# Six weight conversions moved among the early products of experts 1 to 3

## Chip, cores and metric

One core of one Trainium2 chip runs the whole kernel. The metric is device time in microseconds (us), as the median of several executions; the less the better. TensorE does matrix products, VectorE, ScalarE and GpSimd work on vectors, and SyncE issues the transfers (DMAs) between memory and the core's SBUF.

## What is computed

The input is q, k and v of 4 batches, 8 heads, 576 positions and 64 channels. Attention keeps the 32 highest scores of every row. Its output, 2304 rows of 512 channels, goes through 8 experts whose mixing weights are balanced by 8 rounds of Sinkhorn scaling:

```python
scores = scale * np.matmul(q, k.transpose(0, 1, 3, 2))
kth = np.partition(scores, -32, axis=-1)[..., -32:-31]
scores = np.where(scores >= kth, scores, -1e9)
attn = softmax(scores) @ v                       # -> x: (2304, 512)
P = np.exp(x @ w_gate - max)
for _ in range(8):
    P /= P.sum(1, keepdims=True) + 1e-09
    P /= P.sum(0, keepdims=True) + 1e-09
    P *= N / E
for e in range(8):
    out += P[:, e:e + 1] * (np.maximum(x @ w1[e], 0.0) @ w2[e])
```

## The kernel before

The rows of x are cut into blocks of 256 rows (two tiles of 128) by batch and phase; one more block gathers the last 64 positions of the batches. Attention makes these blocks stage by stage (`STAGES`), four head pairs to a stage, and each head pair `hp` fills one of the four 128-deep slices of `xts`, so a product that reads slices 0 and 1 needs head pairs 0 and 1 alone. In attention VectorE finds the 32 highest of each row (`topk`, lines 140 and 143), ScalarE copies scores out of PSUM (line 130) and takes exponentials (148, 149), GpSimd normalises (152, 156) and splits keys and queries, and TensorE does scores (121, 122), transposes (241) and the weighted sums (255, 256). Every finished slice of a block that is due is "boarded": split into a high and a low part, `xh` by ScalarE (line 80) and `xl` by VectorE (line 89).

The experts run as 24 visits, `visit(v, on)` with expert `v % 8`. Visits 0 to 3 have block 0 alone, block 1 boards at visit 4, block 2 at visit 8, and so on. While attention still runs, visits give TensorE work between attention's steps. A visit needs the expert's weights converted: `convert` loads a raw tile `wr`, ScalarE makes the high part `wh` (line 80), GpSimd the low part `wl` (line 86). There are three raw buffers, taken in turn by everything that loads weights, and six buffers each of `wh` and `wl`; a raw buffer is free again when the last reader of its tile is done:

```python
WR, WB, XR, NS, RAW, YB = 3, 6, 3, 3, 3, 4
```

Block 0 has an early part, before its four slices are there. `first_quarter` (products on line 490) multiplies slice 0 with raw weights of experts 4 to 7, one tile to an expert. `first_half` (products on line 502) does slices 0 and 1 for experts 0 to 3, two half tiles `half_weights` to an expert (loads on line 473), with 16 matmul instructions to each half. Both copy their results out by ScalarE (line 478) and store them as partial sums `PART` (line 480). Visits 0 to 3 then need `w1`'s other half only: `second_half` loads the partial sum (line 508), does the products on line 454 and adds (line 514); visit outputs are line 563 and their copies line 571.

The early parts are called from the first stage, ahead of head pairs 1 and 2, at a priority below attention's. The order of instructions on each engine is fixed when the kernel is built, by a planner that weighs priorities and its own estimates of durations. Ahead of head pair 2 stands, before `first_half`, the conversion of all six weight tiles of visit 0: two halves of `w1` and four tiles of `w2` (their loads are on line 436).

Of the kernel before, what the change touches and what calls it, by code (L numbers as in the profile page):

```python
# [48 lines left out]
def kernel(  # L49
# [29 lines left out]
    def hi_act(dst, src):  # L79
        nc.scalar.activation(dst, src, AF.Copy)  # L80
# [4 lines left out]
    def lo_pool(dst, src, hi):  # L85
        nc.gpsimd.tensor_tensor(dst, src, hi.bitcast(F32), op=OP.subtract)  # L86
# [240 lines left out]
    def attend_stage(b, phases, mix):  # L327
        xts = {}
        for ph in phases:
            xts[ph] = xp.tile([128, KD, 256], F32, name="xt", bufs=XR)  # L330
            for t in range(2):
                X["t", b, 2 * ph + t] = xts[ph][:, :, t * 128:(t + 1) * 128]
        xm = None
        if mix:
            m = ("m", b // 2 * 2, b // 2 * 2 + 1)
            if m not in X:
                X[m] = xp.tile([128, KD, 128], F32, name="xm", bufs=2)
                mixed[m] = 0
            xm = X[m][:, :, (b % 2) * 64:(b % 2) * 64 + 64]
            mixed[m] += 1  # L340
        for hp in range(HP):
            if (b, phases) == (0, (0,)) and hp in (1, 2):
                with tc.high_priority(offset=-BIG):
                    if hp == 1:
                        first_quarter(xts[0])
                    else:
                        ready[0] = visit_weights(0)
                        first_half(xts[0])
            attend_heads(b, hp, phases, xts, xm)
        for ph in phases:  # L350
            t = tile_id["t", b, 2 * ph]
            if 2 * b + ph == PARKED:
                nc.sync.dma_start(parked, xts[ph])
            gate_logits(xts[ph], [t, t + 1])
        if mix and mixed[m] == 2:
            gate_logits(X[m], [tile_id[m]])
# [10 lines left out]
    def gate_logits(xt, tiles):  # L367
        lp = pst.tile([128, 512], F32, name="pt")
        for i in range(len(tiles)):
            for kk in range(KD):  # L370
                nc.tensor.matmul(lp[:, i * E:(i + 1) * E], xt[:, kk, i * 128:(i + 1) * 128],
                                 wgs[:, kk * E:(kk + 1) * E], start=(kk == 0), stop=(kk == KD - 1))
        m = len(tiles)
        nc.scalar.activation(lg[:, tiles[0]:tiles[0] + m, :].rearrange("p t e -> p (t e)"),
                             lp[:, 0:m * E], AF.Copy)
# [10 lines left out]
    seats = {i: Seat(xh, xl, hh, hl, i * 256) for i in range(2)}  # L386
# [47 lines left out]
    def convert(src, shape):  # L434
        wr = wp.tile(shape, F32, name="wr", bufs=WR)
        nc.sync.dma_start(wr, src)
        return split_weights(wr, shape)

    def split_weights(wr, shape):
        wh = wp.tile(shape, F32R, name="wh", bufs=WB)  # L440
        wl = wp.tile(shape, F32R, name="wl", bufs=WB)
        hi_act(wh, wr)
        lo_pool(wl, wr, wh)
        return wh, wl

    def products(ps, f0, seat, n, wh, wl, k0):
        nk = wh.shape[1]
        cs = slice(seat.c0, seat.c0 + n)
        for fo in range(512 // n):
            fs = slice((f0 + fo) * 128, (f0 + fo + 1) * 128)  # L450
            i = 0
            for kk in range(nk):
                for a, x in ((wh, seat.xh), (wh, seat.xl), (wl, seat.xh)):
                    nc.tensor.matmul(ps[:, fo, :], a[:, kk, fs], x[:, k0 + kk, cs],  # L454
                                     start=(i == 0), stop=(i == 3 * nk - 1))
                    i += 1
# [13 lines left out]
    def half_weights(e, s2, half):  # L470
        wr = wp.tile([128, 2, 2, 256], F32, name="wr", bufs=WR)
        for r in range(2):
            nc.sync.dma_start(wr[:, r], w1[e, 2 * s2 + r, :, 2 * half:2 * half + 2, :])
        return wr

    def part(e, s, ps):
        y = op_.tile([128, 512], F32, name="y", bufs=YB)
        nc.scalar.activation(y, ps.rearrange("p a b -> p (a b)"), AF.Copy)
        PART[e, s] = dram.tile([128, 512], F32, name=f"p{e}_{s}")
        nc.sync.dma_start(PART[e, s], y)  # L480

    def first_quarter(x):
        for e in LATER:
            wr = wp.tile([128, 4, 256], F32, name="wr", bufs=WR)
            for s in range(4):
                nc.sync.dma_start(wr[:, s], w1[e, s, :, 0, :])
            for s in range(4):
                ps = ps1.tile([128, 2, 256], F32, name="p1")
                for fo in range(2):
                    nc.tensor.matmul(ps[:, fo, :], wr[:, s, fo * 128:(fo + 1) * 128], x[:, 0, :],  # L490
                                     start=True, stop=True)
                part(e, s, ps)

    def first_half(x):
        for e in ALONE:
            for s2 in range(2):
                wr = half_weights(e, s2, 0)
                for r in range(2):
                    ps = ps1.tile([128, 2, 256], F32, name="p1")
                    for fo in range(2):  # L500
                        for kk in range(2):
                            nc.tensor.matmul(ps[:, fo, :], wr[:, r, kk, fo * 128:(fo + 1) * 128], x[:, kk, :],  # L502
                                             start=(kk == 0), stop=(kk == 1))
                    part(e, 2 * s2 + r, ps)

    def second_half(e, s, seat, wh, wl, k0):
        y = op_.tile([128, 512], F32, name="y", bufs=YB)
        nc.sync.dma_start(y, PART[e, s])
        y = y.rearrange("p (a b) -> p a b", a=2)
        ps = ps1.tile([128, 2, 256], F32, name="p1")  # L510
        products(ps, 0, seat, 256, wh, wl, k0)
        ft = slice(2 * s, 2 * s + 2)
        with tc.high_priority(offset=2 * BIG):
            nc.vector.tensor_tensor(ps, ps, y, op=OP.add)
            store_hidden(seat, ft, slice(0, 256), ps)
# [5 lines left out]

    ready = {}

    def visit_weights(e):
        w1s = []
        for s2 in range(2):
            wh, wl = split_weights(half_weights(e, s2, 1), [128, 2, 2, 256])
            w1s += [(wh[:, r], wl[:, r]) for r in range(2)]
        return w1s, [convert(w2[e, s], [128, 2, 512]) for s in range(4)]

    def visit(v, on):
        e = v % E
        ids = [SEAT[blk] for blk in on]
        groups = []
        if on[0] == 0:
            on_first, ids = True, ids[1:]
        else:
            on_first = False
        if 0 in ids and 1 in ids:
            groups, ids = [(seats[0], 512)], [i for i in ids if i > 1]  # L540
        groups += [(seats[i], 256) for i in ids]
        if groups:
            for s in range(4):
                wh, wl = convert(w1[e, s], [128, KD, 256])
                if on_first:
                    second_half(e, s, seats[0], wh[:, 1:4], wl[:, 1:4], 1)
                for seat, n in groups:
                    hidden(seat, n, s, wh, wl)
            ws = [convert(w2[e, s], [128, 2, 512]) for s in range(4)]
        else:  # L550
            w1s, ws = ready.pop(v) if v in ready else visit_weights(e)
            for s, (wh, wl) in enumerate(w1s):
                second_half(e, s, seats[0], wh, wl, 2)
        for blk in on:
            seat = seats[SEAT[blk]]
            for ti, piece in enumerate(BLOCKS[blk]):
                ts = slice(seat.c0 + ti * 128, seat.c0 + (ti + 1) * 128)
                ps = ps2.tile([128, 512], F32, name="p2")
                i = 0
                for ft in range(NFT):  # L560
                    wh, wl = ws[ft // 2]
                    for a, m in ((seat.hh, wh), (seat.hh, wl), (seat.hl, wh)):
                        nc.tensor.matmul(ps, a[:, ft, ts], m[:, ft % 2, :],  # L563
                                         start=(i == 0), stop=(i == 3 * NFT - 1))
                        i += 1
                output(v, tile_id[piece], ps)
# [272 lines left out]
```

## Time and profile before

| | |
|---|---|
| median of 3 runs | 1937.91 us (1937.78 to 1939.51) |
| profiled execution, own time | 1935.34 us |
| its span, first to last instruction | 1933.6 us |
| TensorE busy | 1879.3 us |
| VectorE, ScalarE, GpSimd busy | 1320.0, 1110.0, 1015.6 us |
| mean granted TensorE clock | 0.993 |

The profile is one execution. Times in it count from the first instruction. PE is TensorE (PEld its weight loads, which overlap PE), DVE VectorE, ACT ScalarE, POOL GpSimd, SP SyncE. The granted clock is given as a share of full speed, 2.4 GHz; its other level is 1.2 GHz. `L86` is line 86 of the kernel. In a row, what stands in brackets is how long the engine was idle before it and what ended that idle time.

### The profile page before, as it was taken

The numbers are of one execution on the slowest core, as the hardware profiler recorded it, in microseconds if no ns is written. First come the engines' busy times: TensorE is split into PE (matmuls) and PEld (weight loads), VectorE is DVE, ScalarE is ACT, GpSimd is POOL, SyncE is SP. The second block draws the span as 40 slices with busy tenths as digits, with TensorE's granted clock in tenths as the row PEclk, the third lists the DMA queues.
The fourth block names the chain that finished last, engine by engine and source line by source line (L and its number), as shares of the span: only waits on it lengthen the run. The fifth ranks groups of instructions, "written<-read, shape, count | busy, mean of one in ns | idle before, by whom it ended". The sixth has DMA issues, their size and how long they took to land.

```text
span 1933.6 us, 27187 instructions
## 1 busy us (share of the span) xinstructions
PE 1879.3 (97%) x9649; PEld 1578.9 (82%) x9649; DVE 1320.0 (68%) x2645; ACT 1110.0 (57%) x1929; POOL 1015.6 (53%) x778
## 2 busy tenths in 40 slices
PE   5799999999999999999999999999999999999998
PEld 3577788899888888888888888888888888888886
DVE  8979898999898998289999623135555555543333
ACT  5877777777786877578777654443333333333331
POOL 3537766546545535454435488865555445555440
PEclk9899999999999999999999999999999999999999
DMA  4765554434333334343323225633333333211111
GB/s 126 264 222 176 196 160 151 143 108 161 109 124 124 111 101 132 128 138 126 114 93 122 99 78 194 199 120 104 104 109 114 116 103 104 93 60 56 65 33 44
DMA packets 96073, 237.93 MB, mean 123 GB/s; under 512 B 10816, under 2 KB 15040, under 8 KB 95936
## 3 DMA queue, kind: packets, MB, share of 16 engines
q1 hardware_dynamic: 95936, 236.19, 38.0%
q8 instruction: 76, 1.25, 0.3%
q14 instruction: 61, 0.50, 0.1%
HBM read 201.54 MB, written 34.60 MB: 122 GB/s over the span
## 4 chain that ended last, share of the span: by engine, by line
PE 91%; ACT 2%; DMA 2%; POOL 2%; issue 1%; DVE 1%; SPq 0%; ACTq 0%; POOLq 0%
PE p L563 20%; PE p L454 20%; PE p L733 18%; PE p L674 9%; PE pc L674 5%; PE pt L241 3%; PE pb L674 2%; PE sp L121 2%; PE sp L122 2%; PE pt L255 2%; PE pt L279 2%; PE pt L278 2%; PE p L502 2%; DMA wr<-in_w_dram 1%; POOL wl L86 1%
## 5 line engine op out<-in xcount | busy, mean ns | idle before, releaser
L86 POOL TENSOR_TENSOR wl<-wr,wh 128x1024 fp32r<-128x1024 f32 x280 | 674.6, 2421 | 577.2 <-ACT wh L80 524.9
L80 ACT ACTIVATE wh<-wr 128x1024 fp32r<-128x1024 f32 x280 | 295.5, 1061 | 306.4 <-PE p L674 194.0
L140 DVE MAX8 m<-w 128x8 f32<-128x576 f32 x432 | 319.3, 751 | 3.2
L454 PE MATMUL p<-xh,wh 128*128 128x256 f32 (+1 forms) x800 | 271.4, 340 | 0.8 <-DVE hl L519 0.8
L454 PE MATMUL p<-xh,wl 128*128 128x256 f32 (+1 forms) x800 | 271.1, 339 | 0.0
L454 PE MATMUL p<-xl,wh 128*128 128x256 f32 (+1 forms) x800 | 271.1, 339 | 0.0
L563 PE MATMUL p<-wh,hh 128*128 128x512 f32 x640 | 251.4, 396 | 3.5 <-ACT hh L518 3.5
L563 PE MATMUL p<-wl,hh 128*128 128x512 f32 x640 | 250.9, 395 | 0.0
L563 PE MATMUL p<-wh,hl 128*128 128x512 f32 x640 | 244.9, 395 | 0.0
L143 DVE MATCH_REPLACE8 w<-m,w 128x576 f32<-128x576 f32 x288 | 213.5, 742 | 0.1
L580 DVE SCALAR_TENSOR_TENSOR acc<-p,P,acc 128x512 f32<-128x512 f32 x120 | 89.5, 750 | 166.9 <-PE p L733 166.9
L733 PE MATMUL p<-wh,h2h 128*128 128x512 f32 x512 | 199.8, 391 | 1.3 <-ACT h2h L697 0.7
L733 PE MATMUL p<-wl,h2h 128*128 128x512 f32 x512 | 199.9, 391 | 0.0
L733 PE MATMUL p<-wh,h2l 128*128 128x512 f32 x512 | 196.7, 390 | 0.0
L519 DVE SCALAR_TENSOR_TENSOR hl<-p,hh 128x512 fp32r<-128x512 f32 x160 | 109.0, 683 | 97.0 <-ACT hh L518 95.9
L454 PEld LDWEIGHTS p<-xh,wh 128*128 128x128 f32 x800 | 152.5, 191 | 17.1 <-DVE hl L519 1.3
L454 PEld LDWEIGHTS p<-xl,wh 128*128 128x128 f32 x800 | 152.5, 191 | 15.3
L454 PEld LDWEIGHTS p<-xh,wl 128*128 128x128 f32 x800 | 152.4, 191 | 14.2 <-issue 0.4
L563 PEld LDWEIGHTS p<-wh,hh 128*128 128x128 f32 x640 | 120.4, 189 | 26.6 <-ACT hh L518 4.5
L563 PEld LDWEIGHTS p<-wh,hl 128*128 128x128 f32 x640 | 120.3, 188 | 22.4
L563 PEld LDWEIGHTS p<-wl,hh 128*128 128x128 f32 x640 | 120.6, 188 | 22.0
L140 DVE MAX8 m<-s 128x8 f32<-128x576 f32 x144 | 108.2, 751 | 39.8 <-ACT s L130 24.4
(185 smaller groups left out, 3905.9 us busy)
## 6 DMA issues: line engine op xcount, KB each, us to landing
wr<-in_w_dram SPq DMA_DIRECT2D x240, 512.0 KB, 3.5
y<-y SPq DMA_DIRECT2D x160, 256.0 KB, 2.6
raw<-in_k_dram SPq DMA_DIRECT2D x56, 288.0 KB, 3.2
raw<-in_q_dram SPq DMA_DIRECT2D x32, 256.0 KB, 3.3
p<-y SPq DMA_DIRECT2D x32, 256.0 KB, 4.1
wr<-in_w_dram SPq DMA_DIRECT2D x32, 256.0 KB, 3.5
y<-p SPq DMA_DIRECT2D x32, 256.0 KB, 4.7
raw<-in_v_dram SPq DMA_DIRECT2D x20, 288.0 KB, 3.0
```

The source lines that it names most:

```text
L80: nc.scalar.activation(dst, src, AF.Copy)
L86: nc.gpsimd.tensor_tensor(dst, src, hi.bitcast(F32), op=OP.subtract)
L121: nc.tensor.matmul(o, qc, kh[:, cs], start=(i == 0), stop=False)
L140: nc.vector.max(m8[:, u, r, :], ws[u] if r else units[u][0])
L143: nc.vector.match_replace(ws[u], m8[:, u, r, :], ws[u] if r else units[u][0], LOWEST)
L241: nc.tensor.transpose(ps[:, r, :], Ef[:, o:o + 128], idt)
L454: nc.tensor.matmul(ps[:, fo, :], a[:, kk, fs], x[:, k0 + kk, cs], start=(i == 0), stop=(i == 3 * nk - 1))
L519: nc.vector.scalar_tensor_tensor(seat.hl[:, ft, cs], src, 0.0, seat.hh[:, ft, cs].bitcast(F32), op0=OP.max, op1=OP.subtract)
L563: nc.tensor.matmul(ps, a[:, ft, ts], m[:, ft % 2, :], start=(i == 0), stop=(i == 3 * NFT - 1))
L580: return nc.vector.scalar_tensor_tensor(ACC[t], y, g, ACC[t], op0=OP.mult, op1=OP.add)
L674: nc.tensor.matmul(ps, w[:, kk, :], x[:, kk, :], start=(fresh and i == 0), stop=(i == 5), skip_group_check=True)
L733: nc.tensor.matmul(ps, a[:, ft, ts], m[:, ft, :], start=(i == 0), stop=(i == 11))
```

## The change

The six conversions of visit 0 are no longer made ahead of `first_half`. `first_half` makes them itself and returns them: none behind expert 0, and two behind each of experts 1, 2 and 3. The turn in which tiles take the three raw buffers changes from "experts 4 to 7; six conversions; eight halves of experts 0 to 3" to "experts 4 to 7; two halves of expert 0; two of expert 1; two conversions; two of expert 2; two conversions; two of expert 3; two conversions". `visit_weights(e)` becomes `conversion(e, i)`, which makes one of the six; the other visits without a second block call it six times in the same order as before.

```diff
                     if hp == 1:
                         first_quarter(xts[0])
                     else:
-                        ready[0] = visit_weights(0)
-                        first_half(xts[0])
+                        ready[0] = first_half(xts[0])
...
     def first_half(x):
+        got = []
         for e in ALONE:
             for s2 in range(2):
                 wr = half_weights(e, s2, 0)
...
                     part(e, 2 * s2 + r, ps)
+            if e:
+                got += [conversion(0, 2 * e - 2), conversion(0, 2 * e - 1)]
+        return got
...
-    def visit_weights(e):
-        w1s = []
-        for s2 in range(2):
-            wh, wl = split_weights(half_weights(e, s2, 1), [128, 2, 2, 256])
-            w1s += [(wh[:, r], wl[:, r]) for r in range(2)]
-        return w1s, [convert(w2[e, s], [128, 2, 512]) for s in range(4)]
+    def conversion(e, i):
+        if i < 2:
+            return split_weights(half_weights(e, i, 1), [128, 2, 2, 256])
+        return convert(w2[e, i - 2], [128, 2, 512])
...
-            w1s, ws = ready.pop(v) if v in ready else visit_weights(e)
-            for s, (wh, wl) in enumerate(w1s):
-                second_half(e, s, seats[0], wh, wl, 2)
+            got = ready.pop(v) if v in ready else [conversion(e, i) for i in range(6)]
+            for s in range(4):
+                wh, wl = got[s // 2]
+                second_half(e, s, seats[0], wh[:, s % 2], wl[:, s % 2], 2)
+            ws = got[2:]
```

## Rows read from the trace of the kernel before

**Rows 1.** The page: busy us (share of span) and instructions, by engine.
```profile
PE 1879.3 (97%) x9649; PEld 1578.9 (82%) x9649; DVE 1320.0 (68%) x2645; ACT 1110.0 (57%) x1929; POOL 1015.6 (53%) x778
```

**Rows 2.** Stretches: start:end, length, busy us by engine, granted clock, DMA share, GB/s.
```profile
75.25:85.31 10.06, 1.33 (x5) 0.99 (x5) 10.06 (x24) 9.97 (x17) 8.61 (x6) 0.58 0.84 273
85.31:91.20 5.89, 5.89 (x16) 4.80 (x17) 5.89 (x15) 2.27 (x5) 5.81 (x6) 0.56 0.63 202
91.20:135.33 44.13, 44.13 (x232) 34.97 (x231) 37.54 (x83) 29.34 (x60) 13.41 (x18) 1.00 0.68 221
135.33:253.00 117.67, 112.14 (x634) 88.98 (x633) 103.06 (x222) 89.88 (x163) 84.33 (x64) 0.99 0.59 192
253.00:400.00 147.00, 140.00 (x940) 129.16 (x939) 138.17 (x297) 113.02 (x208) 81.54 (x80) 0.98 0.44 143
400.00:1934.00 1534.00, 1526.19 (x7624) 1284.88 (x7622) 958.34 (x1864) 814.75 (x1384) 795.18 (x578) 1.00 0.34 109
```

**Rows 3.** TensorE's timeline, 72 to 136 us: start, duration, instruction.
```profile
72.27 1.03 PE L490 MATMUL p<-xt,wr 128*128 128x256 f32 x4
...
80.36 0.61 PE L121 MATMUL sp<-kh,qs 128*128 128x288 f32 x1 [5.12 <-ACT s L130]
...
85.31 6.25 PE L502 MATMUL p<-xt,wr 128*128 128x256 f32 x16 [3.62 <-DMA wr<-in_w_dram]
...
115.22 0.40 PE L121 MATMUL sp<-kh,qs 128*128 128x288 f32 x1
...
115.85 3.62 PE L502 MATMUL p<-xt,wr 128*128 128x256 f32 x16
...
135.33 0.47 PE L454 MATMUL p<-xh,wh 128*128 128x256 f32 x1
```

**Rows 4.** Lines 80 and 86, 60 to 100 us: ns min/median/max, first and last start.
```profile
L80 ACT ACTIVATE wh<-wr x6: 1039/1091/1098, 63.6 to 82.6; 128x1024 fp32r<-128x1024 f32 x6
...
L86 POOL TENSOR_TENSOR wl<-wr,wh x6: 2356/2364/2381, 64.8 to 86.7; 128x1024 fp32r<-128x1024 f32 x6
```

**Rows 5.** SyncE's timeline, 46 to 112 us: raw weight loads issued.
```profile
57.73 1.26 SPq L473 DMA_DIRECT2D wr<-in_w_dram  x2
...
65.69 0.81 SPq L473 DMA_DIRECT2D wr<-in_w_dram  x2
...
69.98 0.38 SPq L436 DMA_DIRECT2D wr<-in_w_dram  x1
...
82.63 3.53 SPq L473 DMA_DIRECT2D wr<-in_w_dram  x4
```

**Rows 6.** ScalarE's timeline: head pair 1's slice of x written.
```profile
69.57 0.38 ACT L257 ACTIVATE xt<-pt 128x256 f32<-128x256 f32 x1 [1.50 <-PE pt L256]
```

**Rows 7.** Line 473's 24 loads, 50 to 140 us, from issue to landing.
```profile
DMA to landing us min/median/max: 2.5/3.5/5.2
```

**Rows 8.** VectorE's timeline: boarding of slices, and a top-k step.
```profile
72.51 2.40 DVE L89 TENSOR_TENSOR xl<-xt,xh 128x256 fp32r<-128x256 f32 x1 [1.09 <-ACT xh L80]
...
101.41 0.76 DVE L140 MAX8 m<-s 128x8 f32<-128x576 f32 x1 [1.90 <-ACT s L130]
...
107.78 0.43 DVE L89 TENSOR_TENSOR xl<-xt,xh 128x256 fp32r<-128x256 f32 x1 [2.12 <-ACT xh L80]
...
129.33 0.43 DVE L89 TENSOR_TENSOR xl<-xt,xh 128x256 fp32r<-128x256 f32 x1 [1.75 <-ACT xh L80]
...
236.44 0.36 DVE L89 TENSOR_TENSOR xl<-xt,xh 128x256 fp32r<-128x256 f32 x1
```

**Rows 9.** GpSimd's timeline: a conversion at 72 us.
```profile
72.26 2.37 POOL L86 TENSOR_TENSOR wl<-wr,wh 128x1024 fp32r<-128x1024 f32 x1 [2.83 <-ACT wh L80]
```

**Rows 10.** ScalarE's timeline: the last output of visit 3 copied out.
```profile
253.49 0.60 ACT L571 ACTIVATE y<-p 128x512 f32<-128x512 f32 x1
```

**Rows 11.** TensorE's timeline, 315 to 320 us: two waits.
```profile
315.51 0.55 PE L241 MATMUL pt<-idt,Et 128*128 128x128 f32 x3 [1.38 <-DVE atl L89]
318.58 0.55 PE L241 MATMUL pt<-idt,Et 128*128 128x128 f32 x3 [2.52 <-DVE atl L89]
```

## The prediction

> **What bounds the kernel now.** I began with the page's busy times: TensorE is busy for 1879.3 of the 1933.6 us [rows 1], so only some 54 us can be had by filling its gaps, and a change that adds no arithmetic has to be judged by which gaps it fills. Next, the stretches. From 400 us on TensorE is busy 1526.19 of 1534.00 us; from 91.20 to 135.33 it is busy without a break; the gaps that this diff can touch lie between 75.25 and 91.20 [rows 2]. In the first 10.06 us of that it worked 1.33 us, at a granted clock of 0.58, while VectorE and ScalarE were full [rows 2]. TensorE's timeline names the two gaps: 5.12 us until the scores of head pair 2, whose score buffer had to be copied out first, and 3.62 us until the raw weights of `first_half` landed [rows 3]. Then the clock was still at the lower level (0.56, which is mostly 1.2 GHz): the first 16 products of `first_half` took 6.25 us, and the same 16 took 3.62 us at 115.85 [rows 2, 3].
>
> Why the weights landed so late is told by the conversions and SyncE's queue. Six conversions, each 1.09 us on ScalarE and 2.36 us on GpSimd, ran from 63.6 to 89.1 us [rows 4], and all six stand ahead of `first_half` in the three raw buffers. Loads of the first two were issued at 57.73 and 65.69, of the third at 69.98, and the first load of `first_half` only at 82.63 [rows 5]. Yet the rows that these products read, head pairs 0 and 1, were written at 69.57 + 0.38 = 69.95 us [rows 6]. So there was TensorE work whose inputs were ready some 15 us before its weights.
>
> **What the stretch loses.** 10.06 - 1.33 = 8.73 us idle. The four score products cost 1.33 us there and 0.63 us at full clock (from 115.22 to the next row at 115.85), so 0.70 us. The first 16 products: 6.25 - 3.62 = 2.63 us. Together 12.1 us [rows 2, 3]. From 75.25 to 135.33, where visit 0 begins [rows 3], 60.08 us pass with 48.0 us of full-clock work in them.
>
> **The change, part by part.** *Moved loads and products.* In the three raw buffers expert 0's two halves now stand directly behind experts 4 to 7, where two conversions stood. They inherit those issue slots, 57.73 and 65.69, and with the longest landing of such a load, 5.2 us [rows 5, 7], both are there by 71. Expert 1's first half takes the buffer of expert 7, whose last products ended at 72.27 + 1.03 = 73.30 [rows 3]: it lands by 78.5. Each half is 16 products, 3.62 us; expert 1's second half takes the buffer of expert 0's first, free at about 75.25 + 3.62 = 78.9, and lands by 84.1. So four halves, 14.5 us of work, stand in the stretch that held 8.73 us of gaps, each before it is due. I count the 12.1 us as removed in that place, the clock's part with them since no gap is left to lower it.
>
> *Moved conversions.* The same six pairs of instructions and the same loads, two behind each of experts 1, 2 and 3. No instruction is added: 6 x 1.09 = 6.5 us of ScalarE and 6 x 2.36 = 14.2 us of GpSimd go from the front into 91.20 to 135.33, where GpSimd is busy 13.41 of 44.13 us and ScalarE 29.34 [rows 2]. That room hides them: nil. Without it they would be 14.2 us of GpSimd in front of visit 0. Their last need is late: visit 0's first products at 135.33 less the gain, and the four of `w2` later. The weight values, the store order of the partial sums and the later visits (which get the same six conversions in the same order) are unchanged: nil.
>
> *New waits.* Expert 2's first half must now wait for expert 1's second, and its second half for a conversion; expert 3's likewise. With nothing else to do TensorE would wait a load's landing at each, 3.5 us as the median, 5.2 at most [rows 7]: 7.0 to 10.4 us. Behind such a wait stand, in TensorE's queue, the transposes and scores of head pairs 2 and 3; in ScalarE's the score copies and exponentials behind a conversion whose load is late; in GpSimd's the normalising of weights; in SyncE's the next key and query loads. Attention fills part of it: 48.0 - 8 x 3.62 = 19 us of the stretch's work is not `first_half`.
>
> *What is late next.* Filling the gap does not start visit 0 by itself. Visit 0's first products need head pair 3 boarded, which VectorE ended at 129.33 + 0.43 = 129.76 [rows 8]. If attention runs as before, visit 0 starts 135.33 - 129.76 = 5.6 us earlier and the other 6.5 us become idle time ahead of it. That is the lower bound of the gain in this mechanism. Above it stands what attention may gain: boarding head pair 1 took 2.40 us instead of 0.43, beside a conversion on GpSimd that ran from 72.26 for 2.37 us [rows 8, 9], and it now has no conversion beside it: 1.97 us in an engine that is full. VectorE then waited 1.90 and 2.12 us for score copies and boarding that stood behind late TensorE work [rows 8]. All three would make 6.0 us and the gain 11.6 us. I take the first and not the other two, because conversions now stand in ScalarE's queue in just that stretch and the new waits of experts 2 and 3 resemble the lateness that made them: 5.6 + 1.97 = 7.5 us.
>
> The page "SBUF — State Buffer" of the Trainium skill, section "Who interferes with whom", says that a VectorE instruction with two SBUF inputs and a GpSimd instruction that reads SBUF exclude each other, and the later one waits in full. The 2.40 us row agrees: it ended 0.28 us after GpSimd's. The rule speaks against the change too, since conversions now run while head pair 2 is boarded; if one meets it, the same 1.97 us is lost there and the sum would be 5.6 instead of 7.5.
>
> *Does it last?* Block 1 is boarded at 236.44 + 0.36 = 236.80 and visit 3 ends at 253.49 [rows 8, 10], so visits 0 to 3 may finish up to 16.7 us earlier before they run into it; 7.5 fits. From there on TensorE is nearly never idle [rows 2], so work done earlier shortens the end.
>
> **Rivals.** *A, the above, chance 0.52*: 7.5 us, its own range 5.6 to 9.5.
>
> *B, attention follows all the way, 0.15*: 11.6 us, 1926.3. For it: VectorE's waits named above came from TensorE being late. Against: the conversions in the way. If the new order also loses the two waits at 315.51 and 318.58 (1.38 + 2.52 us [rows 11]), it is 1922.4.
>
> *C, hidden anyway, 0.22*: the head start is idled away before 400 us. For it: from 135.33 to 253 TensorE waits 5.5 us in spite of 95% busy, VectorE is 88% busy and from 253 to 400 it is 94% [rows 2], so attention may set the pace whatever products are done. Then 1937.9, or with a little kept, 1935. Against: the slack of 16.7 us and the full TensorE after 400.
>
> *D, slower, 0.11*: the products of experts 2 and 3 stand in TensorE's queue ahead of attention and their weights are late. Price: two waits of 5.2 us, the low clock after each as at 85.31 (2.63 us), and VectorE starved once as by the 1.90 and 2.12 us: 10.4 + 5.3 + 4.0 = 19.7, against 12.1 won: 7.6 us slower at most, 3.6 without VectorE's part, so about 1943.5. It decides from 12.1 us of new waits on. For it: loads depend on conversions that depend on loads. Against: attention's 19 us lie between them, and TensorE had no break from 91.20 to 135.33 with the same three buffers [rows 2].
>
> **How the numbers follow.** The profiled execution took 1935.34 us by its own time, 1.74 around the span of 1933.6. Less 7.5 gives 1927.8. The median of the runs, 1937.91, stands 2.57 above that execution, so the forecast is 1930.4 us. The range goes down to B with the later waits gone (1922) and up past C to 1939; it leaves out most of D and a little below B. 0.2%, or 3.9 us, is about what a measurement here can tell from no change. A and B are faster by more than that: 0.67. C is the same, with the mild end of D: 0.23. The rest of D is slower: 0.10.
>
> **What would show it.** Right: the products of `first_half` (line 502 before) follow the last of `first_quarter` (line 490) within a few us, no gap over 2 us and no fall of the clock between 75 and 91; conversions on GpSimd between about 85 and 120; visit 0's first product between 124 and 130; the gain still there at 400. The prediction is wrong if TensorE shows waits for raw weights of several us at experts 2 and 3, if the boarding of head pair 3 comes later than 129.8, or if the visits' outputs draw level with before by 400.

## The result and the profile after

The changed kernel takes 1920.80 us (median of 6 runs, 1918.92 to 1921.83) beside 1937.41 us for the kernel before (6 runs, 1933.12 to 1939.51): a ratio of 0.9917, 95% interval 0.9905 to 0.993. It is faster, as forecast, but by 16.6 us instead of 7.5, and 1920.80 lies below the range. The profiled execution took 1921.83 us, its span 1920.1.

The stretches of the changed kernel, cut where its own stages end (columns as in [rows 2]):

```profile
75.25:91.20 15.95, 15.95 (x82) 13.25 (x80) 15.08 (x35) 13.77 (x27) 8.35 (x8) 1.00 0.87 288
91.20:127.29 36.09, 32.77 (x176) 25.35 (x175) 30.49 (x70) 28.67 (x57) 23.25 (x20) 1.00 0.85 288
127.29:253.00 125.71, 117.47 (x666) 95.31 (x667) 115.24 (x247) 96.09 (x173) 91.65 (x67) 0.97 0.59 192
253.00:400.00 147.00, 145.45 (x988) 134.53 (x987) 142.20 (x312) 114.43 (x209) 84.12 (x86) 0.99 0.42 136
400.00:1920.10 1520.10, 1512.68 (x7525) 1272.18 (x7524) 945.08 (x1837) 810.13 (x1371) 787.21 (x569) 1.00 0.35 109
```

The gap of [rows 2] between 75.25 and 91.20 is gone and the clock no longer falls in it. In its place 91.20 to 127.29 has 3.3 us idle. From 253 to 400 TensorE waits 1.55 us where it waited 7.00 [rows 2]: nothing in the forecast's sum says that.

TensorE's timeline of the changed kernel, 72 to 192 us:

```profile
72.55 1.89 PE L502 MATMUL p<-xt,wr 128*128 128x256 f32 x8
75.14 5.34 PE L502 MATMUL p<-xt,wr 128*128 128x256 f32 x24
...
102.60 1.99 PE L502 MATMUL p<-xt,wr 128*128 128x256 f32 x8 [1.01 <-ACT y L477]
...
107.27 3.69 PE L502 MATMUL p<-xt,wr 128*128 128x256 f32 x16 [1.80 <-DMA wr<-in_w_dram]
...
116.17 0.39 PE L453 MATMUL p<-xh,wh 128*128 128x256 f32 x1 [0.25 <-ACT y L477]
...
127.29 0.39 PE L453 MATMUL p<-xl,wh 128*128 128x256 f32 x1 [0.27 <-DVE xl L89]
...
160.24 0.61 PE L121 MATMUL sp<-kh,qs 128*128 128x288 f32 x1 [2.47 <-ACT s L130]
...
189.33 0.40 PE L121 MATMUL sp<-kh,qs 128*128 128x288 f32 x1 [1.78 <-ACT s L130]
```

`first_half` now starts at 72.55 instead of 85.31 [rows 3]. The waits of experts 2 and 3 exist and are small. Visit 0 begins its products of head pair 2's slice at 116.17 and goes on at 127.29, when head pair 3 is boarded; that whole step stood at 135.33 [rows 3]. The two waits at 160 and 189 are new.

VectorE's boardings of head pairs 1, 2 and 3 in the changed kernel, and the first and last of GpSimd's six conversions:

```profile
69.63 0.43 DVE L89 TENSOR_TENSOR xl<-xt,xh 128x256 fp32r<-128x256 f32 x1 [1.91 <-ACT xh L80]
...
96.16 0.40 DVE L89 TENSOR_TENSOR xl<-xt,xh 128x256 fp32r<-128x256 f32 x1
...
126.37 0.87 DVE L89 TENSOR_TENSOR xl<-xt,xh 128x256 fp32r<-128x256 f32 x1
```

```profile
86.98 2.37 POOL L86 TENSOR_TENSOR wl<-wr,wh 128x1024 fp32r<-128x1024 f32 x1 [2.43 <-ACT wh L80]
...
119.50 2.37 POOL L86 TENSOR_TENSOR wl<-wr,wh 128x1024 fp32r<-128x1024 f32 x1
```

Head pair 1's boarding takes 0.43 us instead of 2.40 [rows 8], with no conversion beside it. Head pair 2's, at 96.16, falls between two conversions, of 91.71 and 102.15, and costs 0.40. Head pair 3's takes 0.87, beside two normalisings on GpSimd that run from 126.22 for 1.63 us.

**A table of losses.** For each 5 us of a trace, the length less busy time times granted clock is what TensorE lost, by idling or by a low clock. Summed over stretches this gives, in us, for every profiled execution of this study (the tail behind 1300 us loses 6.0 to 6.3 us in all of them and is not shown):

```
                           median   span | 0-75  75-135 135-255 255-400 400-1300
before                     1937.41 1933.6 | 25.6   12.1     6.9    10.1      3.0
e1_before_again            1937.74 1937.8 | 25.5   12.4     5.4     9.0     10.3
after                      1920.80 1920.1 | 25.5    4.5    11.4     1.9      3.0
e8_after_again             1925.58 1924.9 | 25.4    4.6     9.7     1.4      8.3
e7_w2_first                1941.01 1940.8 | 26.7   11.5     7.2     9.9     11.1
e2_behind_expert0          1935.39 1931.2 | 26.5    8.9     5.3     3.5     11.2
e3_all_last                1933.97 1930.4 | 25.3    6.0     5.7     0.9     17.1
e12_all_last_again         1935.18 1933.6 | 25.1    7.5     9.5     1.0     14.5
e4_own_buffers             1920.36 1921.5 | 34.2    0.0     5.9     1.1      5.9
e5_own_spread              1922.47 1922.8 | 33.0    0.7     5.6     3.6      5.9
e9_own_held                1919.94 1914.4 | 25.2    3.6     6.1     4.0      1.2
e15_held_again             1918.96 1915.4 | 25.4    4.1     6.1     3.7      0.8
e6_wide_gate               1924.17 1923.4 | 27.6    4.1     7.8     8.0      1.1
e14_held_wide_gate         1917.41 1914.6 | 25.8    3.5     6.0     4.1      0.7
e10_five_y_before          1938.18 1931.3 | 25.8   10.4     5.6     9.3      4.6
e11_five_y_after           1923.86 1920.1 | 24.5    5.7     8.0     1.1      4.1
e13_partial_on_scalar      1938.80 1935.4 | 26.1   11.3     6.9    11.2      4.1
e16_early_partial          1931.49 1929.3 | 25.9   11.4     6.8     1.7      7.7
```

Before to after: 12.1 - 4.5 = 7.6 us won in the head (the forecast's 7.5), 4.5 lost again from 135 to 255, 8.2 won from 255 to 400, none from 400 on. The span less all losses is 1869.8 before and 1867.6 after, 2.2 us that this table can't place (the same rest is 1869.2 in e1 and 1869.4 in e8, so the 2.2 us are not shown to be the kernels'). That makes the 13.5 us between the two profiled executions. The other 3.1 us of the 16.6 are that before's profiled execution was 2.07 below its median and after's 1.03 above its own.

### The profile page after: what moved, and what is told of

It is laid out like the page before. It is cut to its first block, busy times and chain, and to the rows that moved or that the text cites. A ratio compares the mean times of both kernels' runs of the same rounds, so it can differ in the third digit from the quotient of the medians.

```text
span 1920.1 us, 27217 instructions
## 1 busy us (share of the span) xinstructions
PE 1874.1 (98%) x9649; PEld 1577.0 (82%) x9649; DVE 1314.6 (68%) x2645; ACT 1112.7 (58%) x1929; POOL 1016.6 (53%) x778
## 3 DMA queue, kind: packets, MB, share of 16 engines
q8 instruction: 76, 1.25, 0.3%
## 4 chain that ended last, share of the span: by engine, by line
PE 88%; DVE 3%; ACT 2%; DMA 2%; POOL 2%; issue 1%; SPq 0%; POOLq 0%; ACTq 0%
PE p L566 20%; PE p L453 19%; PE p L736 18%; PE p L677 9%; PE pc L677 5%; PE pt L241 3%; PE pb L677 2%; PE sp L121 2%; PE sp L122 2%; PE pt L279 2%; PE pt L278 2%; DMA wr<-in_w_dram 2%; PE pt L255 1%; POOL wl L86 1%; DVE m L140 1%
```

## The experiments

### e1, e8: both kernels again

> The kernel before, unchanged, for a second profile. If the waits at 315.51 and 318.58 us and the low clock behind them belong to the fixed order of this kernel, they are there again within 0.5 us each. If they are chance of one execution, the later stretch (135 to 400 us) shows other waits and the span differs from 1933.6 by some us.

> The changed kernel, unchanged, for a second profile. If its losses belong to its fixed order, the stretches 75 to 135, 135 to 255 and 255 to 400 lose 4.5, 11.4 and 1.9 us again within 1.5 each, and only the low clock behind the gate products near 780 and 1120 differs.

Measured: before 1937.74 us, ratio 0.9995 (0.9977 to 1.0013); after 1925.58 us, 0.9923 (0.9898 to 0.9949). The columns up to 400 recur within 2 us in both pairs. The two waits of [rows 11] recur in e1, with 1.30 and 2.50 us. The last column does not recur: 3.0 and 10.3 for one kernel, 3.0 and 8.3 for the other. So the gains up to 400 belong to the kernels and a good part of the rest to the execution.

### e2, e3, e12, e7: another place or order for the six conversions

```diff
-            if e:
-                got += [conversion(0, 2 * e - 2), conversion(0, 2 * e - 1)]
+            if e == 0:      # e2; in e3 and e12: if e == 3
+                got += [conversion(0, i) for i in range(6)]
```

> Expert 0's two halves first, then all six conversions, then experts 1 to 3. If the turn in the three raw buffers decides: 7.2 us of products fill most of the first gap, but experts 1 to 3 wait again behind the conversions from about 82 to 100 us, 3 to 8 us in all; visit 0 starts 2 to 5 us earlier than before, time 1930 to 1935. If it was ScalarE's load of conversions that held the scores of head pair 2: those conversions now run from 80 us on, the 5.1 us wait goes, and most of the gain is there: 1921 to 1927.

> All eight halves first, then the six conversions. If the turn in the raw buffers decides: no gap at 75 to 91 and no wait at experts 2 and 3, the products end 3 us earlier than in the changed kernel, and visit 0 waits for nothing more as long as its first two conversions are done by 120: 1917 to 1922. If the spreading two by two matters: conversions end after 130, visit 0's outputs wait for them, and 3 to 8 us of the gain are lost: 1924 to 1930.

> The kernel with all eight halves first and all six conversions behind them, once more, for a second trace. Theory (its late losses belong to its fixed order): the waits near 422, 954 and 1154 us of about 2.3, 1.2 and 2 us recur, 400 to 1300 loses over 8 us again, and it takes 1933 to 1936 us. Rival (they were an accident of one execution): 400 to 1300 loses 2 to 5 us as in the changed kernel, and its time nears 1924 us.

e7 is the kernel before with `visit_weights(0)` converting the four tiles of `w2` ahead of the two of `w1`.

> The kernel before, but the six conversions (still ahead of all halves) take w2's four tiles first. The gap from 75 to 91 us stays: about 12 us lost from 75 to 135. If the waits at 313 to 330 us in the kernel before are an accident of its fixed order, any new order rolls them anew: 2 to 8 us less lost from 255 to 400, time 1930 to 1936. If they come from visit 0's late start, they stay and the time is 1936 to 1940.

Measured: e2 1935.39 us, 0.9978 (0.9963 to 0.9993); e3 1933.97, 0.9969 (0.9955 to 0.9983); e12 1935.18, 0.9979 (0.9962 to 0.9995); e7 1941.01, 1.0003 (0.9987 to 1.0019). In e7 the gap stays (11.5 us): which of the six comes first does not matter, that they come first does. The stall behind 313 us stays too, with 9.9 us lost from 255 to 400; TensorE's timeline of e7 there:

```profile
315.14 0.55 PE L241 MATMUL pt<-idt,Et 128*128 128x128 f32 x3 [1.40 <-DVE atl L89]
318.62 0.90 PE L241 MATMUL pt<-idt,Et 128*128 128x128 f32 x3 [2.93 <-DVE atl L89]
```

But this run does not separate the two readings that its text gave: from 256 to 330 us TensorE's order in e7 is product for product that of before. In e2 expert 0's products fill the stretch up to 83 us, 8.9 us are lost where it was 12.1, and TensorE's timeline names the longest wait left:

```profile
87.92 1.12 PE L241 MATMUL pt<-idt,Et 128*128 128x128 f32 x4 [4.53 <-POOL Et L156]
```

That is attention's normalising, queued on GpSimd behind a conversion that started at 84.78. e3 has no gap at all up to 91.20 and has lost least of these by 400, and still ends 8 to 13 us behind the two measurements of the changed kernel. TensorE's timeline of its second trace, e12, from 400 to 1160 us, shows why:

```profile
423.61 0.50 PE L566 MATMUL p<-wh,hh 128*128 128x512 f32 x1 [0.88 <-ACT hh L521]
427.07 0.55 PE L453 MATMUL p<-xh,wh 128*128 128x256 f32 x1 [2.26 <-DVE hl L522]
...
957.70 0.50 PE L453 MATMUL p<-xh,wh 128*128 128x512 f32 x1 [1.25 <-DVE hl L522]
1157.65 0.59 PE L426 MATMUL pt<-cs,ones 128*128 128x8 f32 x2 [2.08 <-DVE cs L424]
```

The same four stand in e3 at 419.16, 422.70, 954.47 and 1154.42, with 0.88, 2.35, 1.25 and 2.08 us. So they are of its order, not of one execution, and the changed kernel has none of them: from 400 to 1300 us TensorE idles 7.8 us in e3 and 8.8 in e12, against 1.3 and 1.5 in the two traces of the changed kernel. Moving six conversions makes the planner draw another order hundreds of us behind them, and here that is worth more than half of the gap.

### e4, e5, e9, e15: the conversions out of the ring of raw buffers

```diff
+    def own_conversion(i):
+        if not OWN:
+            OWN.extend(xp.tile([128, KD, 256], F32, name="xt", bufs=XR) for _ in range(2))
+        raw = OWN[i % 2]
...
```

Two tiles of the `xt` ring, idle at that time, hold the raw weights of the six. e4 has them ahead of `first_half` as before; e5 in the places of the changed kernel; e9 and e15 as e5, but each pair's loads stand in SyncE's queue behind the loads of the expert they follow:

```diff
-                got += [own_conversion(2 * e - 2), own_conversion(2 * e - 1)]
+                with tc.issue_after(HELD[0].ins):
+                    got += [own_conversion(2 * e - 2), own_conversion(2 * e - 1)]
```

> The order of the kernel before (six conversions ahead of all halves), but the conversions load into two raw buffers of their own, so that the halves take the three common ones directly behind experts 4 to 7. If the turn in the raw buffers decides: the halves' products follow at 73 us although the conversions still run at 60 to 100, no gap, 1919 to 1926. If the conversions' load on ScalarE and GpSimd at 63 to 89 us held attention: the wait for score copies stays (3 to 5 us) and the gain is less than half: 1929 to 1937.

> The changed kernel's order (two conversions behind each of experts 1, 2, 3), with the conversions loading into two raw buffers of their own. If the changed kernel's loss of 4.5 us from 75 to 135 comes from halves of experts 2 and 3 that wait for raw buffers, it goes: 1 us or less there, and the time falls by 2 to 5 us below 1920.8 unless later stretches take it back. If those waits come from ScalarE's and VectorE's queues, they stay and the time is 1919 to 1923.

> The changed order, the six conversions in two raw buffers of their own as in the run with own buffers and the changed order, but with each pair's loads issued behind the loads of the expert it follows, so that no conversion stands in ScalarE's queue before 75 us. Theory (the head's losses are the turn of the raw buffers and, with own buffers, only conversions that came too early): up to 75.25 TensorE loses about 25.5 us as before and not 31 to 34, at 75 to 135 about 0 to 1, and nothing changes later: about 55 less 6 to 8 us of loss, 1914 to 1917 us. Rival (own buffers do not help once the loads are held: the conversions come as late as in the changed kernel and experts 2 and 3 wait again): 4 us lost at 92 to 135, 1919 to 1923 us. A re-drawn order behind 135 us could hide 4 us of either.

> The kernel with held conversions once more, beside the others on one chip. Theory (its order has fewer waits than the changed kernel's): 1916 to 1920 us, 2 to 5 below the changed kernel's 1921 to 1925. Rival (the first trace of 1914.4 us was a lucky one): 1920 to 1923 us, no different from the changed kernel.

Measured: e4 1920.36 us, 0.9901 (0.9878 to 0.9923); e5 1922.47, 0.9905 (0.9885 to 0.9925); e9 1919.94, 0.9901 (0.9882 to 0.9921); e15 1918.96, 0.9898 (0.9878 to 0.9919). Stretches of e4, and ScalarE's and TensorE's timelines of e4 around 54 us:

```profile
40.00:75.25 35.25, 30.09 (x121) 21.40 (x120) 31.54 (x73) 27.47 (x52) 18.85 (x15) 0.85 0.69 226
75.25:135.00 59.75, 59.75 (x319) 47.34 (x319) 53.58 (x124) 45.04 (x94) 25.18 (x28) 1.00 0.71 231
```

```profile
53.23 1.06 ACT L80 ACTIVATE wh<-xt 128x1024 fp32r<-128x1024 f32 x1 [0.61 <-DMA xt<-in_w_dram]
54.19 0.58 ACT L477 ACTIVATE y<-p 128x512 f32<-128x512 f32 x1
```

```profile
54.82 1.13 PE L489 MATMUL p<-xt,wr 128*128 128x256 f32 x4 [1.78 <-ACT y L477]
```

TensorE has no idle time from 75.25 to 135 in e4, but this does not isolate the turn of the raw buffers. The conversions no longer wait for a buffer, so the first starts at 53.23, and five of the six have left ScalarE by 75.25; before, four of the six ran behind that time. ScalarE waits for their loads, `first_quarter`'s copies behind them hold TensorE, and attention is held up as well. ScalarE's row of head pair 1's slice of x and TensorE's first row of `first_half` in e4:

```profile
79.37 0.38 ACT L257 ACTIVATE xt<-pt 128x256 f32<-128x256 f32 x1 [1.75 <-PE pt L256]
```

```profile
84.28 5.48 PE L502 MATMUL p<-xt,wr 128*128 128x256 f32 x24
```

That slice comes at 79.37 instead of 69.57 [rows 6], and `first_half`, whose first load is now issued at 64.23, starts at 84.28, hardly before the 85.31 of [rows 3] and not at 73 as its text expected. What fills the stretch is `first_quarter` and attention, which were late. e5 went the same way: 0.7 us lost from 75 to 135 but 33.0 ahead of it, and `first_half` at 83.64. Up to 135 us e4 loses 34.2 us and e5 33.7, against 37.7 before and 30.0 in the changed kernel.

The turn of the buffers is shown by the kernel before itself: GpSimd's row of the fourth conversion, and what SyncE's loads of `first_half` waited for from 78 to 90 us (total, times, longest):

```profile
80.22 2.38 POOL L86 TENSOR_TENSOR wl<-wr,wh 128x1024 fp32r<-128x1024 f32 x1
```

```profile
SPq L473 <- POOL wl L86: 3.7, 2, 1.9
```

That conversion ends at 82.60, and the first load of `first_half` is issued at 82.63 [rows 5]. With expert 0's halves ahead of the conversions `first_half` starts at 74.90 in e2, 73.20 in e3 and 72.55 in the changed kernel. How much of the 5.12 us wait for score copies [rows 3] the conversions on ScalarE made, no run separates.

e9 holds the conversions' loads back: the stretch up to 75 loses 25.2 us again and `first_half` starts at 73.10. From 75 to 135 e9 and e15 still lose 3.6 and 4.1 us, as the rival said, and not 0 to 1: the wait for a weight load is gone, and the longest waits left, 1.1 to 1.4 us, are for copies on ScalarE. The two traces lose 46.3 and 46.4 us in all, against 52.5 and 55.5 of the changed kernel. The theory's 1914 to 1917 is met by e9's profiled execution (1916.28), not by the medians, and by the intervals e9 and the changed kernel can't be told apart.

### e10, e11, e13, e16: what stopped TensorE at 315 us before

The rows of the kernel before that bear on [rows 11]: SyncE's queue from 306 us, then VectorE, then TensorE's next wait.

```profile
309.98 0.33 SPq L436 DMA_DIRECT2D wr<-in_w_dram  x1
311.38 0.33 SPq L201 DMA_DIRECT2D raw<-in_v_dram  x1
311.76 0.42 SPq L508 DMA_DIRECT2D y<-p  x1
```

```profile
314.89 0.56 DVE L89 TENSOR_TENSOR atl<-pt,ath 128x384 fp32r<-128x384 f32 x1 [0.50 <-ACT ath L80]
316.71 0.70 DVE L514 TENSOR_TENSOR p<-p,y 128x512 f32<-128x512 f32 x1 [1.26 <-DMA y<-p]
317.32 0.75 DVE L140 MAX8 m<-w 128x8 f32<-128x576 f32 x1
317.98 0.54 DVE L89 TENSOR_TENSOR atl<-pt,ath 128x384 fp32r<-128x384 f32 x1
```

```profile
319.90 0.58 PE L454 MATMUL p<-xh,wh 128*128 128x256 f32 x1 [0.78 <-DVE hl L519]
```

VectorE waits for the partial sum of expert 5 (L508's load, 4.95 us from issue to use); the low part `atl` at 317.98 stands behind it in VectorE's queue, and TensorE's transposes at 318.58 [rows 11] wait for `atl`. Of TensorE's 1.38 + 2.52 + 0.78 = 4.68 us the load's direct part, by these rows, is VectorE's 1.26. Three ways to bring the load earlier were tried on the kernel before, one of them on the changed kernel too (room for a fifth buffer comes from reading one column of ones as a broadcast and from keeping the logits in attention's pool):

```diff
# e10 on before, e11 on after: one more y buffer
-WR, WB, XR, NS, RAW, YB = 3, 6, 3, 3, 3, 4
+WR, WB, XR, NS, RAW, YB = 3, 6, 3, 3, 3, 5
...
# e13 on before: expert 5's four loads issued by ScalarE
-        nc.sync.dma_start(y, PART[e, s])
+        (nc.scalar if e == 5 else nc.sync).dma_start(y, PART[e, s])
...
# e16 on before: the first of the four in a buffer of its own, loaded when it is there
+        if (e, s) == (5, 0):
+            y = EARLY[0]
...
+            EARLY.append(op_.tile([128, 512], F32, name="yq", bufs=1))
+            nc.sync.dma_start(EARLY[0], PART[5, 0])
```

> The kernel before with five instead of four y buffers (room for it from a column of ones read as a broadcast and the logits in another pool); everything up to 300 us stands in the same order on TensorE. Theory (the stall of before at 313 to 330 us is the partial sum's load held up behind outputs that share the four y buffers): no wait over 1 us at 313 to 320, 255 to 400 loses 2 to 4 us instead of 9 to 10, the head keeps its 12 us: about 1931 us. Rival (the load is late for its place in SyncE's queue, or attention is simply late there whatever the buffers): the waits of about 1.4 and 2.5 us recur and it takes 1937 to 1939 us.

> The changed kernel with five y buffers. Theory (the changed kernel has already lost that stall by starting the visits 8 us earlier, so the two savings overlap): 1920 to 1923 us, no gain over the changed kernel. Rival (the stall and the change are independent; the changed kernel still loses to the shared buffers in 135 to 400): 3 to 6 us less, 1916 to 1918 us.

> The kernel before, with the four partial-sum loads of expert 5 alone issued by ScalarE instead of SyncE. TensorE's order is that of before until behind the stall at 313 to 330 us. Theory (the load at 311.76 stood in SyncE's queue behind a weight load that waited 3.5 us for GpSimd and a load of v that waited 1.0): VectorE's wait of 1.26 us for the partial sum and TensorE's 2.52 and 0.78 behind it are gone or under 1 us together, the first wait of 1.38 stays since a conversion on ScalarE makes it, 255 to 400 loses 4 to 7 us instead of 9 to 10: some 3 to 5 us faster, about 1934 us. Rival (attention is late there for GpSimd's sake, the load is only what came last): the waits of about 4 us stay under another releaser, 1937 to 1939 us.

> The kernel before, with the first partial sum of expert 5 loaded into a buffer of its own as soon as it is stored, some 200 us ahead of its use (room as in the run with five y buffers). The load moved to ScalarE was still issued only when the outputs of the visit before were out, and took 5.4 us to land among 400 GB/s of other transfers; this one cannot be late. Theory (the late partial sum is what stops VectorE, and with it TensorE, at 313 to 330 us): VectorE's wait of 1.3 to 1.8 us for the partial sum goes, TensorE's wait of 2.5 us and what follows it fall below 1.5 us together, 255 to 400 loses 3 to 6 us instead of 9 to 11, and it takes 1933 to 1935 us. Rival (GpSimd, busy without a break from 308 to 318, and the weight loads behind it make all of visit 5 late, and the partial sum was only one of the late things): 3 us or more of waits stay at that place under other releasers, 1936 to 1939 us.

Measured: e10 1938.18 us, 0.9991 (0.9977 to 1.0004); e11 1923.86, 0.9924 (0.9903 to 0.9945); e13 1938.80, 1.0002 (0.9988 to 1.0016); e16 1931.49, 0.9959 (0.9946 to 0.9972). VectorE's addition of that partial sum in e13 and in e16:

```profile
316.00 0.70 DVE L514 TENSOR_TENSOR p<-p,y 128x512 f32<-128x512 f32 x1 [1.78 <-DMA y<-p]
```

```profile
315.78 0.69 DVE L517 TENSOR_TENSOR p<-p,y 128x512 f32<-128x512 f32 x1
```

and the stretches around it, first of before, then of e16:

```profile
312.00:320.00 8.00, 3.32 (x25) 2.64 (x24) 6.25 (x14) 6.86 (x15) 7.91 (x5) 0.95 0.92 317
320.00:330.00 10.00, 10.00 (x58) 9.72 (x59) 9.93 (x22) 6.82 (x14) 4.70 (x6) 0.70 0.50 170
```

```profile
312.00:320.00 8.00, 8.00 (x63) 7.71 (x62) 8.00 (x19) 7.59 (x15) 7.32 (x6) 1.00 0.99 341
320.00:330.00 10.00, 10.00 (x77) 9.58 (x76) 9.78 (x20) 7.63 (x15) 6.62 (x6) 1.00 0.49 160
```

The theory of the shared y buffers falls: with five, TensorE still waits 1.44 and 3.08 us there. The theory of SyncE's queue, as e13 put it, falls too: ScalarE issued the load at 310.58, only 1.2 us earlier, and it took 5.4 us to land, so the wait stayed and this run doesn't test the cause. In e16, with this one load issued at 59.68 us, all three waits are gone, the clock stays at 1.00, and 255 to 400 loses 1.7 us instead of 10.1. The kernel is 7.3 us faster than before's median beside it. So the stall can be taken out without moving a conversion. The rival, that GpSimd made all of visit 5 late, finds no support: GpSimd is nearly as full (7.32 of 8.00) and nothing stops.

e16 does not show that the load alone did it. TensorE's order is nearly before's up to 299 us and VectorE's up to 294; behind that, at the place of the stall itself, both are drawn anew. TensorE's transposes there in e16:

```profile
313.60 0.49 PE L241 MATMUL pt<-idt,Et 128*128 128x128 f32 x3
...
317.86 0.49 PE L241 MATMUL pt<-idt,Et 128*128 128x128 f32 x3
```

Between these two groups TensorE has 4 us of products. Before, three products stand ahead of the transposes at 315.51 and none between those and the transposes at 318.58. The wait of 1.38 us, which stands ahead of the load's use, is gone as well. The stall is there in the five traces whose order at that place is before's or nearly so (before, e1, e7, e10, e13), and how much of it the load makes and how much the order stays open.

In the changed kernel the same addition stands at 304.99 without a wait, its load issued at 297.29, 7.7 us ahead, and TensorE has 3.8 us of products between the transposes around it. So the changed kernel's 8.2 us from 255 to 400 are in the main this stall (4.68 us idle and 3.1 at the lower clock before), which the changed kernel does not have; whether its earlier start or its order removes it is not separated. e11 fits: no further gain from more buffers.

### e6, e14: gate products of 64 columns

```diff
-                nc.tensor.matmul(lp[:, i * E:(i + 1) * E], xt[:, kk, i * 128:(i + 1) * 128],
-                                 wgs[:, kk * E:(kk + 1) * E], start=(kk == 0), stop=(kk == KD - 1))
+                nc.tensor.matmul(lp[:, i * 64:(i + 1) * 64], xt[:, kk, i * 128:(i + 1) * 128],
+                                 wgw[:, kk, :], start=(kk == 0), stop=(kk == KD - 1))
...
```

`wgw` holds eight copies of the gate weights, of whose products one is read. e6 is the changed kernel, e14 is e9 with this edit.

> The changed kernel, but every gate product streams 64 columns (8 copies of the 8 gate weights) instead of 8; the values copied out are the same. The runs of 32 narrow products near 780 and 1120 us keep TensorE busy without a gap, and yet the granted clock falls to the lower level behind them. If their narrowness does that, the low clock behind them is gone, the mean clock rises and the time falls by 1 to 5 us. If it is chance or has another cause, the low clock stays there and the time is 1920.8 within 1.5.

> The held conversions in buffers of their own, and the gate products streaming 64 columns (eight copies of the same gate weights, of which one is read), so their values stay. Theory (narrow products let the clock fall in any order): no low clock behind the gate products near 785 and 1140 us, at most 0.5 us of low clock in 400 to 1300; 2 to 4 us less than the held kernel where the new order of instructions brings no wait, 1916 to 1918 us. Rival (what is won there is lost to a re-drawn order as in the first run with wide gate products): 1920 to 1924 us.

Measured: e6 1924.17 us, 0.9921 (0.9902 to 0.994); e14 1917.41, 0.9888 (0.9869 to 0.9906), the lowest of the study. Stretches of e8 and of e14 around a run of 32 gate products, which start at 778.13 in e8 (4.58 us) and at 780.91 in e14 (3.68 us):

```profile
778.00:782.50 4.50, 4.50 (x34) 4.46 (x32) 3.97 (x9) 0.18 (x1) 1.81 (x1) 0.79 0.53 180
782.50:785.00 2.50, 2.50 (x8) 1.91 (x8) 0.00 (x0) 0.18 (x1) 0.00 (x0) 0.50 0.08 30
785.00:787.50 2.50, 2.50 (x10) 2.11 (x9) 0.00 (x0) 0.66 (x2) 0.00 (x0) 0.52 0.00 0
```

```profile
778.00:782.50 4.50, 4.50 (x29) 3.97 (x28) 4.37 (x8) 1.82 (x3) 1.11 (x1) 1.00 0.00 0
782.50:785.00 2.50, 2.50 (x22) 2.41 (x22) 0.27 (x2) 0.37 (x2) 1.24 (x1) 1.00 0.08 18
785.00:787.50 2.50, 2.50 (x15) 2.06 (x14) 0.00 (x0) 0.66 (x2) 0.00 (x0) 1.00 0.54 198
```

TensorE is busy without a gap in both, by the profile's rows, and with 8 columns the clock is at its lower level, 1.2 GHz, behind them. Neither trace with 64 columns loses anything to the clock from 400 to 1300 us. e6 gains nothing by it, since its new order has a wait of 3.76 us at 369.96 and 8.0 us of loss from 255 to 400. e14 brought no such wait, but e9 and e15, with 8 columns, happened to lose nothing to the clock there either. The times say a little more: e14's six lie within 2.6 us, e9's and e15's within 5.4 and 6.8. The mean granted clock of each execution points the same way: 0.998 or 0.999 in e14's six, 0.995 to 0.999 in the twelve of e9 and e15; in e6's six it is 0.995 to 0.998. By the intervals e14 is not told apart from e9 and e15, and that the narrow products lower the clock is not shown.

## Why the prediction was wrong

*The gap and its clock* (12.1 us lost there, removed): right. 15.95 of 15.95 us busy at 1.00. The cause that the prediction gave, the turn of the raw buffers, stands in before's own rows: a load issued 0.03 us behind the end of a conversion. e4, which was to test it alone, did not.

*Four halves, each before it is due*: right; the products go from 72.55 on, and no wait stands in front of 102.60.

*Moved conversions at nil*: right for this placing. e2 shows the price without cover: 4.53 us of waiting for GpSimd in one place.

*New waits of experts 2 and 3*, bounded by 10.4 us: they are 1.01 and 1.80, with 4.5 us lost from 75 to 135 in all. Rival D falls. The forecast left 12.1 - 7.5 = 4.6 us idle ahead of visit 0 and nothing at these experts; it is in part luck that the 4.5 us, which stand elsewhere, agree with it.

*Visit 0 when head pair 3 is boarded, 5.6 + 1.97 = 7.5 us*: right. Its first products stand at 116.17, earlier than the 124 to 130 given, but the rest starts at 127.29, 8.0 us earlier than before, against a forecast of 127.8; the boarding of head pair 1 costs 0.43. So rival A's mechanism held in the head: attention did not follow by the 11.6 us of B, and nothing was idled away as in C. The page "SBUF — State Buffer" of the Trainium skill, section "Who interferes with whom", would have cost the 1.97 again if a conversion had met head pair 2's boarding; none did (0.40 us), so no row tests it there. Head pair 3's boarding, beside the two normalisings of 126.22, took 0.87 us instead of 0.43, which goes the same way.

*Does it last?* This is the step that failed. The prediction held that the diff can touch only the gaps between 75.25 and 91.20, and that from the end of visit 3 TensorE is nearly never idle, so work done earlier shortens the end. From 400 on that held. Between 135 and 400 it gave the change no term, though [rows 2] had 5.5 and 7.0 us idle there; measured, 4.5 us were lost and 8.2 won. The prediction had the stall's rows ([rows 11]), but put them into rival B alone, as 1.38 + 2.52 us for the case that attention follows all the way. The stall is not tied to that: it went with 7.6 us of head start, and with none at all in e16. And it was priced without what follows it, 0.78 us more of waiting and 3.1 us at the lower clock. That the 8.2 us would be won could not be read from before alone. That a wait stood behind one load with 4.95 us from issue to use could, and with the whole stall gone B alone would have been 1926.3 - 8.2 = 1918.1, below the range. The stall is not all of the miss: of the 9.1 us more than forecast, 8.2 - 4.5 = 3.7 come from 135 to 400, 2.2 have no place, and 3.1 are the medians against the profiled executions.

*The median*: the forecast carried over that before's median stood 2.57 us above its profiled execution. After's stood 1.03 below, and the pair of medians moved by 3.1 us more than the pair of traces. The variable part lies from 400 on, 3.0 to 10.3 us of loss in the same kernel. How much of the 3.1 us recurs stays open: e8's ratio gives 14.9 us, the first measurement 16.6.

What also stays open is why 135 to 255 loses more after. Both traces of the changed kernel idle 7.1 us there, against 5.5 and 5.4 before, and the lower clock costs 4.3 and 2.6 us against 1.4 and 0.0. The rows show ScalarE copying scores late, at 159.55, behind two weight conversions at 155.81 and 157.51; no run took this apart, though e9 and e15 lose 6.1 there instead of 9.7 to 11.4.

## What to carry to other kernels

When several stages take buffers from one ring, look at who stands ahead in the ring and not only at who is busy: a load whose work could start at once may be queued behind tiles that are first needed tens of us later. Where the order on every engine is fixed ahead by a planner, an early edit can redraw it far behind; list the transfers of the later stages that are issued only about one landing time ahead of their use, since each may be a stall that the edit removes or brings. And measure an edit's own term in its own stretch (7.6 us here, 7.5 forecast, in part by luck) before believing that the whole difference (16.6) is its doing.

## What the runs showed of the hardware

The granted clock fell to 0.50 to 0.52 behind runs of 32 products of 8 columns although TensorE was busy without a gap before it and after it. It did so in some executions and not in others (0 to 8.6 us lost behind such runs from 400 to 1300 in kernels with 8 columns), and in neither trace with 64 columns; e9 and e15, with 8, lost nothing either, so the narrow products are a suspect and not a shown cause. This part differs by 6.9 us between the two traces of the kernel before and by 5.1 between those of the changed one, whose spans differ by 4.2 and 4.8.
